# Attention and a gated feed-forward block in one kernel: turning some queries of batch 1 by DMA, turning 64-token tiles without their unused rows, and moving batch 2's scaling

## The chip, the cores and the metric

The kernel runs on one core of one Trainium2 chip. Times are device microseconds of that core; a profile is one execution of its own, and its span is about 2 us shorter than the time. A ratio is the mean time of one kernel's fast runs over the mean of the other's in the same rounds, so it is not quite the ratio of the medians that are quoted.

## The reference

```python
# 8 batches, 8 heads, 576 tokens, head dimension 64
def phi(x, c, s):                       # c, s: cos and sin of the token's position
    r = np.maximum(x, 0.0)
    return np.concatenate([r * c, r * s], axis=-1)
q_p, k_p = phi(q, cos_w, sin_w), phi(k, cos_w, sin_w)
kv  = np.einsum('bhsf,bhsd->bhfd', k_p, v)
num = np.einsum('bhsf,bhfd->bhsd', q_p, kv)
den = np.einsum('bhsf,bhf->bhs', q_p, k_p.sum(axis=2))[..., None] + 1e-06
x   = (num / den)                       # then [4608 tokens, 512]
g   = x @ w_gate                        # [512, 1536]
out = (gelu(g) * (x @ w_val)) @ w_out   # [1536, 512]
```

## The kernel before

A batch has 576 tokens: tiles 0 to 3 of 128 tokens and tile 4 of 64, which lie in the even rows of a 128-row tile. Scaled queries must be turned (features onto partitions) to be the stationary operand of the numerator; the normalised activations must be turned to feed the feed-forward block. Batches 0 and 1 turn theirs on TensorE, batches 2 to 7 by DMA. The feed-forward part runs in blocks of 512 tokens (block 0 has 576, the last 448), and the attention of the next batch is woven into a block. A "unit" is one call of `gv_unit`. To evacuate is to copy a result out of PSUM, the memory that TensorE writes.

```python
def turn_q(b, j0, j1):                  # queries, by DMA
    nc.sync.dma_start_transpose(out=qT[b % 2][:, j0:j1]..., in_=qp[:, j0:j1]...)

def numer_mm(b, t, bank, g, rows=128):
    for h in range(4 * g, 4 * g + 4):
        nc.tensor.matmul(ps[0:rows, bank + g, ...],
            lhsT=qT[b % 2][:, t, h, 0:rows], rhs=kv[b % 2][:, h, 0:D + 1], ...)

def turn_x(b, t, xb):                   # activations, by DMA
    if t < NJ:
        nc.sync.dma_start_transpose(out=xT[:, :, p0:p0 + 128], in_=xb2)
    else:                               # 64 tokens: turned with the unused rows, then picked out
        xr = rot.tile([128, CT, 128], BF16, name="xr")
        nc.sync.dma_start_transpose(out=xr, in_=xb2)
        nc.gpsimd.tensor_copy(xT[:, :, p0:p0 + 64], xr[:, :, 0:128:2])

def gv_unit(n, jt, c0, w, gb, vb):      # gate: 4 matmuls, gelu; value: 4 matmuls, product
    ...
```

The stretch that the change touches, the end of block 0 and the start of block 1 (`sq`, `sk` scale a tile of queries or keys; `o_tile` is an output tile; `x_by_pe`, `q_by_pe` turn on TensorE and copy out of PSUM):

```python
sq(4, 0, "v"), sq(4, 1, "s")
load_q(2)
...
o_tile(0, 1, 5)
q_by_pe(1, 2, 6, "v"); q_by_pe(1, 3, 7, "s")
cast_v(1, 0, 4, "v"); cast_v(1, 4, 8, "s")
load_v(2)
sq(0, ...), sq(1, ...), sq(2, 0, "v")          # of batch 2
o_tile(0, 2, 4)
q_by_pe(1, 4, 2, "v")
kv_half(1, 0, 6, "s"); kv_half(1, 1, 7, "v")
sq(2, 1, "s"), sq(3, 1, "s"), sq(4, 1, "s"); turn_q(2, 0, 3)
...
```

All transfers from `nc.sync` go through one queue, in program order; in this kernel's trace none of its 153 that were recorded landed before the one issued ahead of it.

## Time and profile before

| | before |
|---|---|
| time, median | 331.8 us (331.4 to 332.2) |
| span of the profile | 329.8 us |
| TensorE's share of the chain that ended last | 92% |
| from block to block (blocks 2 and on) | 33.77 us |
| block 2's first matmul | 86.69 us |

TensorE is the bound nearly everywhere, so a change is worth what it takes out of TensorE's stream or adds to it.

### The profile page before, as it was taken

Reading aid. Unit: us, or ns where it says so; the run is one execution under the profiler, and the core shown is the slowest. Engines: PE = TensorE matmul, PEld = TensorE weight load, DVE = VectorE, ACT = ScalarE, POOL = GpSimd, SP = SyncE. Lnnn points to the kernel's source line nnn. Section 1 sums busy time; section 2 is a strip of 40 time slices with the busy share of each in tenths; the row PEclk is TensorE's granted clock in tenths of the full one; section 3 lists DMA queues with packets and bytes.
Section 4 is the critical chain, followed back from the end, with each engine's and each line's share of the span. In section 5 each row is a group of like instructions: output and inputs, shape, how many; then the busy total and the mean of one; then the engine's idle time right before and its main releaser. Section 6 shows DMA issues by size and latency. Waiting matters only on the chain.

```text
span 329.8 us, 5965 instructions
## 1 busy us (share of the span) xinstructions
PE 319.8 (97%) x2245; PEld 170.7 (52%) x2280; DVE 173.3 (53%) x392; ACT 155.9 (47%) x283; POOL 19.7 (6%) x39
## 2 busy tenths in 40 slices
PE   7899999999999999999999999999999999999995
PEld 2578766655445444544454445444554444444443
DVE  5975477867664548354835474557545232222210
ACT  6864479683465247523752276226632223322321
POOL 2350010000100000000100010001000100000000
PEclk9999999999999999999999999999999999999998
DMA  7999999999289936994599549973723121000024
GB/s 231 264 170 207 220 342 329 299 242 312 54 137 265 319 80 114 274 329 84 94 279 298 119 84 218 370 121 73 167 49 80 22 59 32 32 34 33 33 64 97
DMA packets 84381, 54.66 MB, mean 166 GB/s; under 512 B 49408, under 2 KB 79872, under 8 KB 84352
## 3 DMA queue, kind: packets, MB, share of 16 engines
q1 hardware_dynamic: 78128, 49.10, 58.9%
q0 software_dynamic: 5792, 4.72, 9.4%
q10 hardware_dynamic: 432, 0.46, 0.4%
q8 instruction: 18, 0.29, 0.4%
q14 instruction: 11, 0.09, 0.1%
HBM read 37.75 MB, written 9.44 MB: 143 GB/s over the span
## 4 chain that ended last, share of the span: by engine, by line
PE 92%; DVE 2%; DMA 2%; ACT 1%; issue 1%; POOL 0%; DVEq 0%; POOLq 0%; ACTq 0%
PE ps L213 28%; PE ps L245 28%; PE ps L222 27%; PE ps L151 3%; PE ps L167 3%; DMA kf<-in_k_dram 2%; PE ps L310 1%; DVE qp L132 1%; PE ps L263 1%; ACT kp L134 1%; PE ps L329 1%; DVE kp L132 1%; ACT xT L332 0%; ACT gel L218 0%; DVE xb L182 0%
## 5 line engine op out<-in xcount | busy, mean ns | idle before, releaser
L226 DVE TENSOR_TENSOR hT<-gel,ps 128x512 bf16<-128x512 f32 (+5 forms) x130 | 76.9, 596 | 132.6 <-PE ps L222 126.7
L213 PE MATMUL ps<-xT,wg_sb 128*128 128x512 bf16 (+5 forms) x506 | 113.1, 342 | 1.5 <-ACT xT L332 0.5
L222 PE MATMUL ps<-xT,wv_sb 128*128 128x512 bf16 (+5 forms) x508 | 113.0, 342 | 0.8 <-DVE hT L226 0.4
L218 ACT ACTIVATE gel<-ps 128x512 f32<-128x512 f32 (+5 forms) x130 | 68.1, 525 | 78.2 <-PE ps L213 75.0
L245 PE MATMUL ps<-wo_sb,hT 128*128 128x512 bf16 x413 | 95.6, 379 | 0.6
L222 PEld LDWEIGHTS <-wv_sb 128*128 128x128 bf16 x520 | 48.8, 98 | 45.7 <-issue 0.5
L213 PEld LDWEIGHTS <-wg_sb 128*128 128x128 bf16 x520 | 47.0, 98 | 40.3 <-issue 1.2
L245 PEld LDWEIGHTS <-hT 128*128 128x128 bf16 x420 | 40.1, 98 | 45.4
L274 ACT COPY o_sb<-ps 128x512 f32<-128x512 f32 x35 | 20.5, 585 | 74.5 <-PE ps L245 70.2
L182 DVE TENSOR_TENSOR xb<-ps,rec 128x512 bf16<-128x512 f32 (+2 forms) x41 | 27.8, 678 | 1.5
L134 ACT ACTIVATE kp<-kf,sin_c 128x512 bf16<-128x512 f32 (+1 forms) x41 | 25.3, 680 | 1.0 <-DMA kf<-in_k_dram 1.0
L132 DVE TENSOR_SCALAR qp<-qf,cos_c 128x512 bf16<-128x512 f32 (+1 forms) x45 | 21.5, 521 | 0.7 <-DMA qf<-in_q_dram 0.7
L167 PEld LDWEIGHTS <-qT 128*128 128x128 bf16 (+1 forms) x320 | 15.2, 98 | 9.0 <-issue 1.7
L134 ACT ACTIVATE qp<-qf,sin_c 128x512 bf16<-128x512 f32 (+1 forms) x31 | 19.2, 665 | 0.7 <-DMA qf<-in_q_dram 0.7
L132 DVE TENSOR_SCALAR kp<-kf,cos_c 128x512 bf16<-128x512 f32 (+1 forms) x45 | 18.0, 450 | 1.4 <-DMA kf<-in_k_dram 1.4
L167 PE MATMUL ps<-kv,qT 128*128 128x65 bf16 (+1 forms) x320 | 16.7, 194 | 0.1
L206 POOL COPY xT<-xr 128x256 bf16<-128x256 bf16 x6 | 2.4, 400 | 204.0 <-DMA xr<-xb 204.0
L124 PE MATMUL ps<-junk 128*128 128x512 bf16 x34 | 10.7, 471 | 1.8 <-DVE par_i L101 1.7
L151 PEld LDWEIGHTS <-kp 128*128 128x128 bf16 x320 | 10.8, 97 | 2.4 <-issue 1.4
L151 PE MATMUL ps<-vx,kp 128*128 128x65 bf16 x320 | 11.1, 193 | 0.1
L138 ACT CAST vx<-vf 128x1280 bf16<-128x1280 f32 (+1 forms) x9 | 10.7, 1194 | 0.2 <-DMA vf<-in_v_dram 0.2
L231 POOL COPY hT<-hT 128x768 bf16<-128x768 bf16 x8 | 7.6, 946 | 38.1 <-DVE hT L226 38.1
(55 smaller groups left out, 93.5 us busy)
## 6 DMA issues: line engine op xcount, KB each, us to landing
out_dram<-o_sb SPq DMA_DIRECT2D x38, 128.0 KB, 2.4
qf<-in_q_dram SPq DMA_DIRECT2D x7, 640.0 KB, 5.9
kf<-in_k_dram SPq DMA_DIRECT2D x7, 640.0 KB, 7.7
out_dram<-o_sb SPq DMA_DIRECT2D x16, 256.0 KB, 3.5
vf<-in_v_dram SPq DMA_DIRECT2D x6, 640.0 KB, 9.3
qf<-in_q_dram SPq DMA_DIRECT2D x7, 512.0 KB, 4.7
kf<-in_k_dram SPq DMA_DIRECT2D x7, 512.0 KB, 6.4
vf<-in_v_dram SPq DMA_DIRECT2D x6, 512.0 KB, 8.4
```

The costliest lines, as they stand in the source:

```text
L124: nc.tensor.matmul(ps[:, bank, :], lhsT=junk[:, 0:128], rhs=junk, start=True, stop=True)
L132: nc.vector.tensor_scalar(d, s, col, 0.0, op0=ALU.mult, op1=ALU.max)
L134: nc.scalar.activation(d, s, AF.Relu, scale=col)
L151: nc.tensor.matmul(ps[:, bank, (h % 4) * (D + 1):(h % 4 + 1) * (D + 1)], lhsT=kp[:, j, h, :], rhs=vx[b % 2][:, j, h, 0:D + 1], start=(j == ...
L167: nc.tensor.matmul(ps[0:rows, bank + g, (h % 4) * (D + 1):(h % 4 + 1) * (D + 1)], lhsT=qT[b % 2][:, t, h, 0:rows], rhs=kv[b % 2][:, h, 0:D ...
L182: nc.vector.tensor_tensor(xb[0:rows, g0:g1], nd[:, :, :, 0:D], rec[0:rows, 0:n, :, None].to_broadcast([rows, n, 4, D]), op=ALU.mult,)
L213: nc.tensor.matmul(ps[:, gb, 0:w], lhsT=wg_sb[:, ct, jt * 128:(jt + 1) * 128], rhs=xT[:, ct, p0:p0 + w], start=(ct == 0), stop=(ct == CT - 1),
L218: nc.scalar.activation(gel[:, 0:w], ps[:, gb, 0:w], AF.Gelu)
L222: nc.tensor.matmul(ps[:, vb, 0:w], lhsT=wv_sb[:, ct, jt * 128:(jt + 1) * 128], rhs=xT[:, ct, p0:p0 + w], start=(ct == 0), stop=(ct == CT - 1),
L226: nc.vector.tensor_mul(hT[n % 2][:, jt, 64 + c0:64 + c0 + w], gel[:, 0:w], ps[:, vb, 0:w])
L245: nc.tensor.matmul(ps[:, bank, :], lhsT=hT[n % 2][:, jt, c0:c0 + 128], rhs=wo_sb[:, jt, :], start=(jt == 0), stop=(jt == JT - 1),)
L274: nc.scalar.copy(o_sb, ps[:, bank, :])
```

## The change

Three things are meant to help. Tiles 2 to 4 of batch 1's queries are turned by DMA, queued behind v, so that TensorE is spared 24 transposes. Tiles of 64 tokens use only their 64 columns in the numerator (at stride 2), so their result can be turned straight into place. Batch 2's query scaling must then wait for that DMA turn, and moves among block 1's first units.

```diff
-                lhsT=qT[b % 2][:, t, h, 0:rows],
+                lhsT=qT[b % 2][:, t, h, 0:128:2] if t == NJ and b else qT[b % 2][:, t, h, 0:rows],
@@ turn_x
-        if t < NJ: ...dma_start_transpose(out=xT[:, :, p0:p0 + 128], in_=xb2)
-        else: xr = ...; dma_start_transpose(out=xr, in_=xb2); gpsimd.tensor_copy(...)
+        rows = 128 if t < NJ else 64
+        nc.sync.dma_start_transpose(
+            out=xT[:, :, p0:p0 + rows], in_=xb[0:rows].rearrange("p g h d -> p (g h d)"))
@@
     sq(4, 0, "v"), sq(4, 1, "s")
+    turn_q(1, 2, 5)
     load_q(2)
@@
-    q_by_pe(1, 2, 6, "v")
-    q_by_pe(1, 3, 7, "s")
-    sq(0, 0, "v"), sq(0, 1, "s")  ... all of batch 2's sq, turn_q(2, ...), load_q(3)
-    q_by_pe(1, 4, 2, "v")
@@ now after x_by_pe(1, 0), x_by_pe(1, 1), numer(1, 3), numer(1, 4):
+    sq(0, ...)   sq(1, ...)   sq(2, ...), turn_q(2, 0, 3)
+    sq(3, ...), sq(4, ...), turn_q(2, 3, 5), load_q(3)
@@
-            turn_x(b, i - 1, numer(b, i - 1, 6))
+            turn_x(b, i - 1, numer(b, i - 1, 6, 128 if i <= NJ else 64))
```

More of the change, by code (lines that the diff above doesn't have):

```diff
@@ L199, in turn_x @@
         p0 = b * S + t * 128
-        xb2 = xb.rearrange("p g h d -> p (g h d)")
-        if t < NJ:
-            nc.sync.dma_start_transpose(out=xT[:, :, p0:p0 + 128], in_=xb2)
-        else:
-            xr = rot.tile([128, CT, 128], BF16, name="xr")
-            nc.sync.dma_start_transpose(out=xr, in_=xb2)
-            nc.gpsimd.tensor_copy(xT[:, :, p0:p0 + 64], xr[:, :, 0:128:2])
+        rows = 128 if t < NJ else 64
+        nc.sync.dma_start_transpose(
+            out=xT[:, :, p0:p0 + rows], in_=xb[0:rows].rearrange("p g h d -> p (g h d)"),
+        )
     def gv_unit(n, jt, c0, w, gb, vb, mid=()):
@@ L462 @@
     load_v(2)
-    sq(0, 0, "v"), sq(0, 1, "s")
-    sq(1, 0, "v"), sq(1, 1, "s")
-    sq(2, 0, "v")
     o_tile(0, 2, 4)
-    q_by_pe(1, 4, 2, "v")
     kv_half(1, 0, 6, "s")
     kv_half(1, 1, 7, "v")
-    sq(2, 1, "s"), sq(3, 1, "s"), sq(4, 1, "s")
-    turn_q(2, 0, 3)
     y0, y1 = new_xb(), new_xb()
@@ L479 @@
     norm(y1, 2, 0, 2)
-    sq(3, 0, "v"), sq(4, 0, "v")
-    turn_q(2, 3, 5)
-    load_q(3)
     o_part(0, 3, 5, 2, 6)
@@ L485 @@
     x_by_pe(1, 0, y0, 0, "s")
+    sq(0, 0, "v"), sq(0, 1, "s")
     o_part(0, 3, 5, 6, 9)
     x_by_pe(1, 1, y1, 1, "s")
+    sq(1, 0, "v"), sq(1, 1, "s")
     o_part(0, 3, 5, 9, 12)
     y3 = numer(1, 3, 2)
+    sq(2, 0, "v"), sq(2, 1, "s")
+    turn_q(2, 0, 3)
     gv_unit(1, 0, 0, 128, 0, 4)
@@ L495 @@
     y4 = numer(1, 4, 2, 64)
+    sq(3, 0, "v"), sq(4, 0, "v"), sq(3, 1, "s"), sq(4, 1, "s")
+    turn_q(2, 3, 5)
+    load_q(3)
     gv_unit(1, 1, 128, 128, 1, 5)
```

## The prediction

> **What bounds the kernel now.** I read the page first (busy shares, slices, chain), then the chain and the timeline from 44 to 90 us, where the change acts, then a table of stretches and the landings of the transfers.
>
> ```profile
> PE 319.8 (97%) x2245; PEld 170.7 (52%) x2280; DVE 173.3 (53%) x392; ACT 155.9 (47%) x283; POOL 19.7 (6%) x39
> PE   7899999999999999999999999999999999999995
> DMA  7999999999289936994599549973723121000024
> PE 92%; DVE 2%; DMA 2%; ACT 1%; issue 1%; POOL 0%; DVEq 0%; POOLq 0%; ACTq 0%
> ```
>
> TensorE holds 92% of the chain and is never under nine tenths after slice 3. A saving must therefore be matmul time removed or a TensorE gap closed. From block 2 on the chain repeats every 33.77 us (the 40 matmuls of the key-value product at 102.40, 136.18, 169.95, 203.72): pure matmul pace, where nothing off TensorE shows. Block 2 begins at 86.86: its first output tile starts at 90.31, after two units of 1.73.
>
> The second row to see is DMA. In the stretches (columns: us, busy of PE, PEld, DVE, ACT, POOL, clock, DMA share, GB/s):
>
> ```profile
> 50.00:62.00 12.00, 11.89 (x149) 7.88 (x150) 9.83 (x25) 9.79 (x17) 0.00 (x0) 1.00 1.02 353
> 62.00:70.00 8.00, 7.54 (x72) 5.01 (x71) 5.74 (x17) 5.99 (x13) 0.00 (x0) 1.00 1.21 187
> 70.00:81.00 11.00, 10.78 (x103) 5.86 (x104) 7.81 (x16) 5.49 (x10) 0.00 (x0) 1.00 1.17 346
> 81.00:85.00 4.00, 4.00 (x34) 2.10 (x33) 3.31 (x8) 1.20 (x2) 0.00 (x0) 1.00 0.72 110
> 88.00:92.00 4.00, 4.00 (x19) 1.85 (x19) 3.31 (x8) 2.78 (x5) 0.70 (x1) 1.00 0.00 0
> ```
>
> From 50 to 81 us the transfer queue has no free time: q, k, v of batch 2 (50 to 62), the two query turns of batch 2 (62 to 69.4), q, k, v of batch 3 (to 81). It falls idle only after 87. What ends this run of transfers are the turned activations of batch 2, which block 2's first matmul reads (its 512 tokens end inside tile 3 of batch 2):
>
> ```profile
> L202 SPq DMA_TRANSPOSE xT<-xb x4: 1188/1204/2103, 77.0 to 83.0; - x4
> DMA to landing us min/median/max: 2.4/3.5/5.9
> ```
>
> The first was issued at 76.95 and landed 5.9 later, at 82.7, because the loads of batch 3 were ahead of it. In the trace's landings the next two follow at 83.2 and 83.7; the fourth, issued at 82.96, is free of the queue and lands at 85.25. Block 2 starts at 86.86, so the slack is 1.6 us.
>
> **What the Trainium skill says.** "VectorE: DVE Perf Modes", The three transpose paths, gives 390 ns for a 128x128 transpose on TensorE and 1309 ns by DMA. Here pipelined ones cost far less on TensorE (0.89 us for 16, 56 ns each); by DMA, 24 blocks issued into an idle queue at 91.71 landed 6.8 us later. "DMA: Bandwidth & Descriptors", Issuing engines are not separate DMA queues, says that all DMAs share 16 engines and interleave; the trace agrees in that the 57.50 turn waited behind v. "TensorE: Matmul & The Clock Gate", Weight-path perf modes, says fast weight load needs all 128 columns. The trace shows 64-column loads at 110 ns against 98, but the same pace of matmuls (31 to 33 ns). "Advanced Engine Details and Errata", SBUF Cachelines, warns of strided reads; no weights of stride 2 are loaded in this trace, so their price is open.
>
> **The change, part by part.**
>
> (1) 24 TensorE transposes of batch 1 go.
>
> ```profile
> 51.68 0.89 PE ps L310 x16
> 55.16 0.45 PE ps L310 x8
> ```
>
> 0.89 + 0.45 = 1.34 us off the chain. The four copies out of PSUM go too: of VectorE 0.69 (tile 2) and 0.69 (tile 4), of ScalarE 1.01 (tile 3); both engines then finish the casts of v sooner, so the key-value product can follow at once.
>
> (2) In their place one DMA turn of tiles 2 to 4, issued when the last scaling ends, at 48.6. v of batch 1 lands at 49 to 50, so the turn moves from about 49.9. It is the same size as the one at 91.71 (3 tiles), 5.6 to 6.8 us to landing in two steady blocks: landing 54.2 to 55.4. Its first reader, the numerator of tile 2, is at 58.8 now and 57.4 after: hidden, with 2 us to spare.
>
> (3) But it takes the queue. 3072 rows of 256 bytes move at 0.84 to 1.13 per ns, 2.7 to 3.6 us, and where a turn follows loads the packets show a pause of about 1.3 us (62.5 to 63.5, 81 to 82). I take 4.2 us. The load of q of batch 2 comes behind it on the same issuer, whose turn instruction holds it some 4 us:
>
> ```profile
> 48.26 1.31 SPq L78 DMA_DIRECT2D qf<-in_q_dram  x2
> 57.50 7.03 SPq L142 DMA_TRANSPOSE qT<-qp  x1
> ```
>
> q of batch 2 then starts moving at 54.2 instead of 50.0, and everything behind it in the gapless queue slides by as much. Queue-bound landings of batch 2's activations become 82.7 + 4.2 = 86.9, 87.4, 87.8, and the fourth about 88.3. Block 2's first matmul then waits until 88.3 to 88.4 against 86.86: **+1.5 us** at that point, whatever TensorE won before.
>
> (4) Batch 2's query scaling moves. q of batch 2 lands about 54.2 + 4.4 = 58.6 (it took 4.4 from first packet, 50.0, to the first reader's start, 54.38). VectorE asks for it about 59.6: no wait, perhaps a short one. ScalarE is worse: five scalings of 0.72 (3.6 us) ran at 54.7 to 58.6 and now sit among the evacuations and gelus of the first units. Laying them out in program order from 58.7: evacuation of x 1 by 60.6, store copy by 61.9, third scaling 62.6, two gelus 63.2, evacuations of x 2 and 3 with a gelu between 64.7, last two scalings 66.1, gelu 66.4. The unit that reuses that gelu's bank began at 65.65 before and cannot now before 66.4. So the 1.34 us of (1) is gone by 66 and 0.8 us more with it. This is not added to (3): both must be past before block 2, and the later (3) sets it.
>
> (5) The 64-row numerator in batches 2 to 7. Eight matmuls keep their pace, but a change of the array's shape costs TensorE its run-ahead loading:
>
> ```profile
> 63.63 0.33 PEld L167 LDWEIGHTS <-qT 128*64 128x64 bf16 x8
> 64.00 0.23 PEld L213 LDWEIGHTS <-wg_sb 128*128 128x128 bf16 x4
> ```
>
> Around this only such group of batch 1, the matmul starts are 149 ns apart going in (55 inside the group before) and 126 coming out (33 inside): 0.094 each, 0.19 for both. Six batches: 6 x 0.19 = **+1.1 us**, all in the matmul-bound blocks. If loading at stride 2 is slow, up to 48 x 30 ns = 1.4 more; I put no size on it.
>
> (6) Turning 64 rows straight into place takes away six GpSimd copies of 0.40 and half the rows of six small turns. Their data is read a block later: 0.
>
> Sum: 331.8 + 1.5 + 1.1 = 334.4. I shade it to 334.0, since the slide in (3) rests on one queue's estimate.
>
> **Rivals.**
>
> (A) The author's case: all 1.34 us kept, the turn and the moved scalings hidden, no cost in (5): 330.5. For it: TensorE is the bound, 92% of the chain. Against: the DMA row of nines up to 81 us and the 1.6 us of slack at block 2, and the measured 0.19 of a shape change.
>
> (B) ScalarE sets block 1 but the queue does not bind block 2 (say the turn takes only 2.7 us with no pause; then the fourth landing is at 86.8 and block 2 is on time): 331.8 + 0.8 + 1.1 = 333.7. For it: the pauses in the packets come irregularly. Against: four turns in the trace had one.
>
> (C) The slide is larger, since the turn holds the issuer for 7 us as at 57.50, and the turned queries of batch 2 come close to their first reader (landing about 72 now predicted, reader at 74.7): with 6 us of slide block 2 starts at 90, 331.8 + 3.3 + 1.1 = 336.2; slow strided loads would add to it.
>
> (D) Scaling is hidden and the queue is not bound, only (1) and (5): 331.8 - 1.34 + 1.1 = 331.6.
>
> **Range and chances.** The four rivals lie between 330.5 and 336.2; I weigh the main path and (B) most, (C) and (D) less, (A) least. Range 331.2 to 336.6. Two per cent are 6.6 us, more than any sum here: within 2% 0.95, slower 0.04, faster 0.01.
>
> **What would show it.** (1): 56 transposes of queries instead of 80. (2): no wait of the numerators for the DMA turn around 57. (3): the batch 2 activations landing at 87 to 88.5, a TensorE gap of 1 to 2 us before block 2's first matmul that names this DMA, and the q, k, v loads of batch 2 starting 4 us later. (4): ScalarE busy without gaps from 59 to 70, and TensorE gaps there of 1 to 2 us in all that name the gelu. (5): a period of 33.96 instead of 33.77 from block to block. I am wrong if the period is unchanged or longer by over 0.3, if block 2 starts before 86.9, or if TensorE waits for the turned queries.

## More of the kernel before

A transfer has landed when the last of its completion signals has come.

The prediction shows the lines. The one it left out is block 2's first matmul itself (timeline, TensorE; start, duration, engine and line):

```profile
86.69 1.03 PE L213 MATMUL ps<-xT,wg_sb 128*128 128x512 bf16 x4
```

## The result, and the profile after

The changed kernel took 335.78 us in the median of five runs (335.39 to 338.39), against 331.8; the ratio is 1.0133 (95% interval 1.0093 to 1.0174). It is 4.0 us slower, inside the predicted range (331.2 to 336.6), and nearly twice the predicted loss of 2.2.

The page of the changed kernel, the lines that answer to those of before (busy time, TensorE and DMA in 40 slices, the chain by engine):

```profile
PE 320.5 (96%) x2221; PEld 169.5 (51%) x2256; DVE 169.0 (51%) x390; ACT 154.6 (46%) x282; POOL 16.9 (5%) x33
PE   7899999799799999999999999999999999999995
DMA  7999999999858955994499449992924021000024
PE 86%; DMA 5%; DVE 3%; ACT 3%; issue 2%; SPq 1%; POOL 0%; DVEq 0%; ACTq 0%; POOLq 0%
```

TensorE's row has two new dips, in its eighth and eleventh slice (58 to 67 and 83 to 92 us). Everything else of the row is as it was. The stretches of the changed kernel (columns as in the prediction):

```profile
50.00:62.00 12.00, 10.57 (x122) 6.42 (x123) 8.41 (x23) 6.71 (x12) 0.00 (x0) 1.00 1.00 276
62.00:70.00 8.00, 7.54 (x70) 5.16 (x71) 5.86 (x18) 7.39 (x18) 0.00 (x0) 1.00 1.14 302
70.00:81.00 11.00, 10.83 (x104) 5.87 (x105) 7.57 (x16) 5.63 (x11) 0.00 (x0) 1.00 1.07 273
81.00:85.00 4.00, 4.00 (x32) 1.96 (x31) 2.86 (x8) 0.94 (x3) 0.00 (x0) 1.00 1.08 360
88.00:92.00 4.00, 2.62 (x12) 1.29 (x14) 2.16 (x5) 1.21 (x2) 0.82 (x1) 1.00 0.20 40
```

From 81 to 85 the queue now moves 360 GB/s where it moved 110: loads that were over by 81 are still running. TensorE loses 1.3 us from 50 to 62 and 1.4 us from 88 to 92. The transfer queue's own timeline shows who stands in front (SPq is the issuer, the duration is how long the instruction held it):

```profile
48.89 3.73 SPq L142 DMA_TRANSPOSE qT<-qp  x1
52.67 1.29 SPq L78 DMA_DIRECT2D qf<-in_q_dram  x2
62.90 10.26 SPq L142 DMA_TRANSPOSE qT<-qp  x2
```

q of batch 2 is issued at 52.67 instead of 48.26. In the trace the new turn lands at 54.5, in good time for its reader (tile 2's numerator, at 57.1). But q lands too late for its readers:

```profile
59.83 0.72 ACT L134 ACTIVATE qp<-qf,sin_c 128x512 bf16<-128x512 f32 x1 [1.30 <-DMA qf<-in_q_dram]
61.08 0.38 PE L210 MATMUL ps<-xT,wg_sb 128*128 128x128 bf16 x4 [0.79 <-ACT xT L329]
62.17 0.38 PE L219 MATMUL ps<-xT,wv_sb 128*128 128x128 bf16 x4 [0.71 <-ACT o_sb L271]
62.96 0.38 PE L210 MATMUL ps<-xT,wg_sb 128*128 128x128 bf16 x4 [0.18 <-ACT gel L215]
```

The brackets are the idle time ahead of an instruction and what ended it. ScalarE stands 1.30 us waiting for q; the evacuations and gelus behind that scaling come late, and TensorE waits for each in turn. Counted from the starts of the matmuls, TensorE's gaps there are 0.95, 0.88, 0.35 and 0.11 us, 2.3 in all.

At block 2, the four turns of batch 2's activations, who waited for them, and the first matmul:

```profile
L201 SPq DMA_TRANSPOSE xT<-xb x4: 1218/1956/3652, 77.9 to 85.7; - x4
  DVE xb L182: 3.1, 1
  PE ps L210: 2.0, 1
DMA to landing us min/median/max: 3.4/5.4/9.7
```
```profile
89.33 1.02 PE L210 MATMUL ps<-xT,wg_sb 128*128 128x512 bf16 x4 [1.95 <-DMA xT<-xb]
```

The first turn takes 9.7 us from issue to landing instead of 5.9; the four land at 87.5, 88.0, 88.5 and 89.1. TensorE was ready at 87.2 and starts at 89.33: block 2 begins 2.64 us later than before.

Last, the block period, by the 40 matmuls of a batch's key-value product in the chain, before and then after:

```profile
102.40 1.36 PE ps L151 x40
136.18 1.36 PE ps L151 x40
```
```profile
105.03 1.36 PE ps L151 x40
139.03 1.36 PE ps L151 x40
```

33.78 us became 34.00. The span's growth of 3.9 us is then: 2.64 at block 2; four more blocks of 0.225 (0.90); 0.15 in the last batch; and one wait of 0.2 for VectorE in batch 6's numerator at 216.8.

### The profile page after: what moved, and what is told of

Same layout as the page of the kernel before. It is cut to its first block, busy times and chain, and to the rows that moved or that the text cites. A ratio compares the mean times of both kernels' runs of the same rounds, so it can differ in the third digit from the quotient of the medians.

```text
span 333.7 us, 5904 instructions
## 1 busy us (share of the span) xinstructions
PE 320.5 (96%) x2221; PEld 169.5 (51%) x2256; DVE 169.0 (51%) x390; ACT 154.6 (46%) x282; POOL 16.9 (5%) x33
## 4 chain that ended last, share of the span: by engine, by line
PE 86%; DMA 5%; DVE 3%; ACT 3%; issue 2%; SPq 1%; POOL 0%; DVEq 0%; ACTq 0%; POOLq 0%
PE ps L210 27%; PE ps L242 26%; PE ps L219 26%; PE ps L151 3%; PE ps L167 3%; DMA qf<-in_q_dram 2%; DMA kf<-in_k_dram 2%; DMA xT<-xb 1%; DVE qp L132 1%; ACT kp L134 1%; PE ps L260 1%; PE ps L307 1%; ACT qp L134 1%; DVE kp L132 1%; DVE xb L182 1%
## 5 line engine op out<-in xcount | busy, mean ns | idle before, releaser
L228 POOL COPY hT<-hT 128x768 bf16<-128x768 bf16 x8 | 6.8, 852 | 248.7 <-DVE hT L223 248.7
L132 DVE TENSOR_SCALAR qp<-qf,cos_c 128x512 bf16<-128x512 f32 (+1 forms) x45 | 18.9, 463 | 0.3 <-DMA qf<-in_q_dram 0.3
L163 ACT CAST kv<-ps 128x260 bf16<-128x260 f32 x15 | 5.7, 378 | 7.7 <-PE ps L151 7.7
```

The source lines that it names most:

```text
L132: nc.vector.tensor_scalar(d, s, col, 0.0, op0=ALU.mult, op1=ALU.max)
```

## The experiments

The theory: one queue carries everything, so the added turn delays all behind it (the waits at 60 and at 89); and a 64-column tile switches the array's shape, which costs TensorE 0.2 us per batch. The rivals: weights at stride 2 are slow; VectorE, held by a buffer, delays block 2; the moved scaling is what costs. All runs gave a correct result unless said otherwise.

### e2: the 64-column tile alone

```diff
 (on the kernel before)
-    lhsT=qT[b % 2][:, t, h, 0:rows],
+    lhsT=qT[b % 2][:, t, h, 0:128:2] if t == NJ and b > 1 else qT[b % 2][:, t, h, 0:rows],
 and turn_x, numer(..., 64) as in the change
```

> The kernel before with one part of the change alone: the numerator of tile 4 in batches 2 to 7 with 64 columns at stride 2, and the turn of 64 rows straight into place. My theory (each switch of the array's shape costs 0.1 us, two per batch, nothing else in the part costs or wins): the block period goes from 33.77 to about 34.0 us and the time from 331.8 to 333.0 to 333.3. Rival, that the part is free or wins (fewer rows turned, no copy by GpSimd) and the whole loss of the changed kernel lies in block 1: 331.8 or less, period 33.77.

333.18 us in the median (332.42 to 334.87) against 331.47, ratio 1.0064 (1.0033 to 1.0095). The period is 34.00 us in each block. The part that looked like pure saving is a loss. The weight loads of one such tile, kernel before and then the changed one (timeline of weight loads, block 3):

```profile
118.28 0.50 PEld L167 LDWEIGHTS <-qT 128*128 128x128 bf16 x8
```
```profile
121.21 0.33 PEld L167 LDWEIGHTS <-qT 128*64 128x64 bf16 x8 [0.42 <-issue]
```

With 128 columns the first load slips in under the matmul before it, and no idle time is shown. With 64 columns (128\*64 is the shape) the loads stand idle for 0.42 us first. The starts of the matmuls show what of this counts: 0.09 us going into the shape (309 ns from start to start where 216 is usual) and 0.09 coming out (126 where 33 is). Another 0.03 lies right behind these two gaps (53 ns where 29 is usual, 226 where 215 is), which makes up the 0.225 by which the period grew.

### e6: the same 64 columns, side by side

```diff
 (on the changed kernel; a wrong result on purpose)
-    lhsT=qT[b % 2][:, t, h, 0:128:2] if t == NJ and b else qT[b % 2][:, t, h, 0:rows],
+    lhsT=qT[b % 2][:, t, h, 0:rows],
```

> The changed kernel, but the 64 columns of tile 4 are read side by side and not at stride 2 (a wrong result on purpose: the wrong queries). My theory, that the shape of the array costs and not the stride: same time as the changed kernel, 335.8, same period of 34.0 us, gaps of 0.10 us going in and coming out. Rival, that weights at stride 2 are slow: the period falls to 33.8 and the time by 1.0 to 1.4 us.

The result is wrong. 336.61 us in the median (334.91 to 338.43), ratio 1.0152 (1.0100 to 1.0203). The period is 34.00 us again, with the same two gaps of 0.09. So the stride costs nothing; the shape does. The four runs fall into two pairs: 334.9 and 335.3 at a mean clock of 1.0, and 338.0 and 338.4 at 0.995. The last section comes back to that.

### e3: one load moved out of the way

```diff
 (on the changed kernel)
-            put(5 + s, L(load_v, b + 1))
+            if n > 1:
+                put(5 + s, L(load_v, b + 1))
         for i in range(5):
             put(6 + (n == 1) + s + i, L(attn_step, b, i + 1))
+            if n == 1 and i == 3:                  # behind the turn of tile 3
+                put(6 + 1 + s + i, L(load_v, b + 1))
```

> The changed kernel with one load moved in the transfer queue: v of batch 3 is issued behind the turn of tile 3 of batch 2 instead of ahead of the four turns. My theory, that the full queue delays the turned activations and those hold block 2: the turns land by 86 and block 2 starts at about 87.2 us when TensorE is ready for it, not at 89.3; the time falls from 335.8 to 333.5 to 334.0. Rivals: if ScalarE's moved scalings or the wait of VectorE for a buffer were what delays block 2, its start stays at 89 and the time at 335.8.

333.53 us (332.87 to 334.38), ratio 1.0059 (1.0038 to 1.0081). That is 2.2 us under the changed kernel's median (of other rounds; its ratio was 1.0133), by the order of the queue alone. The turns land at 85.2 to 86.6, and block 2's first matmul has no wait in front of it:

```profile
87.44 1.03 PE L210 MATMUL ps<-xT,wg_sb 128*128 128x512 bf16 x4
```

### e4: a fifth buffer for the activations

```diff
 (on the changed kernel)
-        return rot.tile([128, 2, 4, D], BF16, name="xb", bufs=4)
+        return rot.tile([128, 2, 4, D], BF16, name="xb", bufs=5)
```

> The changed kernel with five buffers for the normalised activations instead of four, so that tile 4 of batch 2 need not wait for the turn of its tile 0: it removes the 3.07 us in which VectorE waits for that turn at 84.5 to 87.6. My theory: TensorE waits for the last turn itself, so block 2 still starts at 89.3 and the time stays at 335.8 (at most 0.3 less). Rival, that VectorE's held products are what TensorE waits for: block 2 starts near 87.2 and 2 us are won.

336.72 us (334.66 to 337.16), ratio 1.0142 (1.0108 to 1.0175). VectorE's wait is gone, TensorE's is not:

```profile
85.10 0.68 DVE L182 TENSOR_TENSOR xb<-ps,rec 64x512 bf16<-64x512 f32 x1
```
```profile
90.40 0.81 PE L210 MATMUL ps<-xT,wg_sb 128*128 128x512 bf16 x3 [2.50 <-DMA xT<-xb]
```

The 3.1 us of VectorE was the longest wait in the list of that transfer, and it cost nothing. The buffer rival falls.

### e7: the price of the turn alone

```diff
 (on the kernel before)
     load_v(2)
     ...
+    nc.sync.dma_start_transpose(                    # 24 blocks of weights, into unused columns
+        out=xT[:, 0, 1536:4608].rearrange("p (a t) -> p a t", t=128),
+        in_=wg_sb[:, 0:2].rearrange("p c j -> p (c j)"),
+    )
     turn_q(2, 0, 3)
```

> The kernel before with one transfer added and nothing else touched: a turn of the size of the one that the change adds (24 blocks of 128 by 128, of weights, into columns of the activations that are not yet in use), issued behind v of batch 2. It measures the price of the turn to the transfer queue alone. My theory: everything behind it lands 3 to 4.5 us later, the fourth turn of batch 2's activations at 87.5 to 88.5, block 2 starts 1.3 to 2.3 us later than in the kernel before (86.7), the time is 333.0 to 334.0 and the period of 33.77 us stays. Rival, that the queue has slack or that the extra turn runs beside the loads: 331.5.

333.23 us (332.88 to 334.76), ratio 1.0058 (1.0038 to 1.0078). With no instruction of the four compute engines changed, block 2 waits:

```profile
89.95 1.02 PE L213 MATMUL ps<-xT,wg_sb 128*128 128x512 bf16 x4 [2.76 <-DMA xT<-xb]
```

The turns land at 88.2 to 89.7 in that profile and the period stays 33.77. The profiled execution was the slowest of the four (334.76), so its 3 us are at the upper end; the median lost 1.7.

### e5: TensorE turns the queries again, the rest of the change stays

```diff
 (on the changed kernel)
-    turn_q(1, 2, 5)
+    q_by_pe(1, 2, 6, "v"); q_by_pe(1, 3, 7, "s")    # after o_tile(0, 1), as before
+    q_by_pe(1, 4, 2, "v")                           # after o_tile(0, 2), as before
 (and tile 4 of batch 1 is read at 0:rows again)
```

> The changed kernel with tiles 2 to 4 of batch 1 turned by TensorE again (the DMA turn and its place in the queue are gone, the 24 transposes and four copies are back); batch 2's scaling stays among block 1's first units and tile 4 stays 64 columns wide. My theory: q of batch 2 lands at 54 again, so the waits for it at 59.8 go; ScalarE's moved scalings still cost some 0.5 to 0.9 us against the kernel before in block 1; block 2 starts at 87.2 to 87.9; time 333.3 to 334.3, of which 1.2 for the 64 columns. Rival, that the moved scaling and not the turn is the main loss of block 1 and block 2: 335 or more.

332.82 us (332.70 to 332.96), ratio 1.0036 (1.0024 to 1.0049), and the least scatter of all. q is there when ScalarE asks for it (timeline of ScalarE):

```profile
59.41 0.72 ACT L134 ACTIVATE qp<-qf,sin_c 128x512 bf16<-128x512 f32 x1
60.03 0.58 ACT L329 COPY xT<-ps 128x512 bf16<-128x512 bf16 x1
```

From batch 1's key-value product to batch 2's took 16.97 us, against 16.55 before: the moved scaling costs 0.4 us by itself. The 64 columns (period 34.00) cost most of the rest. Block 2 does not wait. The time lies half a microsecond under what was expected.

### e1: tile 4 back at 128 columns

```diff
 (on the changed kernel) turn_x and numer of batches 2 to 7 as in the kernel before
```

> The changed kernel with tile 4 of batches 2 to 7 handled as in the kernel before (128 columns, turned whole, copied by GpSimd). My theory: the period returns to 33.77 us, the wait at block 2 stays (a start at 89 to 90.5), the time falls by 1.0 to 1.3 us, to 334.5 to 335.5. Rival, that the two parts of the loss are not independent: the gain is under 0.5 us.

335.35 us (335.18 to 336.89), ratio 1.0125 (1.0102 to 1.0148). The period returns to 33.78. The median is only 0.4 us under the changed kernel's, which by itself looks like the rival; but the two are of different rounds, and e4 and e6, which differ from the changed kernel in nothing that counts, took 336.7 and 336.6. In this profile the turns landed at 88.4 to 89.9 and block 2 began at 90.17, 0.8 later than in the changed kernel's: a stretch that ends with a transfer scatters with that transfer. All four runs of e1 also show a lowered mean clock (0.993 to 0.995), where the changed kernel's lay between 0.990 and 1.0; the last section says what that is. The period settles the 64 columns' cost; this run's time does not.

### e8: the two costs taken away together

```diff
 (on e1) load_v as in e3
```

> The changed kernel with two of its costs taken away at once: tile 4 of batches 2 to 7 back at 128 columns, and v of batch 3 behind the turns of batch 2's activations. What is left of the change is the DMA turn of batch 1's queries and the moved scaling. My theory (the costs add): no wait at block 2, period 33.77 us, and only the waits for q of batch 2 in block 1 (2 to 3 us in all) less the 1.34 us of transposes: 332.0 to 332.9, that is 0.5 to 1.3 us slower than the kernel before. Rival, that the parts were not the whole of the loss: over 333.5; rival, that the turn wins once the queue is put right: under 331.3.

333.36 us (331.56 to 334.07), ratio 1.003 (0.9995 to 1.0066). The period is 33.78 and block 2 does not wait. The time lies above what was expected: the waits for q in block 1 remain (gaps of 0.94, 0.88, 0.35 and 0.10 us), and in the profiled execution the clock was halved for 3.4 us right behind them, as in e1. The runs part along that line: three with a mean clock of 0.995 took 333.6 to 334.1 us, three with 0.998 to 1.0 took 331.6 to 333.1, 332.4 in the mean, which is what was expected. The turn of batch 1's queries wins nothing even with the later queue put right.

### b1: no shape but 128 by 128 anywhere

```diff
 (on the kernel before)
-            xs[t] = numer(0, t, 0, 128 if t < NJ else 64)
+            xs[t] = numer(0, t, 0)
-    y4 = numer(1, 4, 2, 64)
+    y4 = numer(1, 4, 2)
 q_evac copies all 128 columns; x_by_pe turns 128 rows and copies every second column
```

> The kernel before with the two remaining tiles of 64 tokens (tile 4 of batches 0 and 1) given 128 columns and 128 rows in the numerator and in the transposes, so that the array's shape is never switched. My theory: eight switches of 0.09 us go, 0.75 us, and eight transposes become 64 columns wider, 0.2 us back: 0.5 us faster than the kernel before, if these switches are not hidden in waits of block 0 and 1 anyway. Rival, that they are hidden there: no difference.

331.78 us (331.32 to 333.55) against 331.52, ratio 1.0012 (0.9993 to 1.003). No gain. Blocks 0 and 1 have waits for ScalarE and VectorE of their own; a saving inside them was not visible here.

### b2 and b3: a version with the queue in mind

```diff
 (b2, on b1)
     load_q(2)
+    turn_q(1, 2, 5)                  # behind q of batch 2, not ahead of it
-    q_by_pe(1, 2..4)
     sq(0), sq(1) of batch 2 before the numerators; sq(2) to sq(4) later, as in the change
     y2 = numer(1, 2), y3 = numer(1, 3) after the last o_part
     load_v as in e3
 (b3, on b2)
-    kv_half(1, 1, 7, "v")
+    kv_half(1, 1, 7, "s")
-    y3 = numer(1, 3, 2)              # ahead of block 1's first two units
+    y3 = numer(1, 3, 2)              # behind them
```

> A try at a version that beats both: the DMA turn of batch 1's queries stays, but q of batch 2 is issued ahead of it; the numerators of tiles 2 and 3 come after the last part of the output tile, so that the later landing of the turn (about 58.5 us) is not waited for; two of batch 2's scalings go back before the numerators; v of batch 3 goes behind the turns of batch 2; all tiles are 128 columns wide. My theory: 24 transposes less (1.3 us) with no wait for q, period 33.77 us, block 2 starts near 86: 330.3 to 331.2. Rival, that the one queue is too full for any extra turn in this stretch (something else then arrives late): 332 or more.

b2: 331.72 us (330.55 to 332.15) against 331.67, ratio 0.9987 (0.9952 to 1.0023). It no longer loses, and does not win: the transposes' 1.3 us went into waits of 0.3 to 0.8 us for VectorE and ScalarE in block 1's first units.

> The reordered try once more, with two of its remaining TensorE waits taken out: the second half of the key-value product is evacuated by ScalarE ahead of batch 2's scalings (it waited behind VectorE's scalings), and the numerator of tile 3 comes after block 1's first two units, so that their products are not held behind its normalisation. My theory: some 0.5 to 0.9 us less than the reordered try (331.7), 330.6 to 331.3, that is at most 0.3 per cent faster than the kernel before, within what five rounds can just tell. Rival, that ScalarE or the landing of the turn takes over the wait: 331.7 again.

b3: 330.94 us (330.18 to 332.05) against 331.75, ratio 0.9974 (0.9945 to 1.0002). In the median it is 0.8 us faster than the kernel before, and it beats the changed kernel by far, but the interval just touches 1: likely a small win, not shown.

## Why the prediction was right or wrong

It was right in direction and range, and in the mechanism of its two main terms, (3) and (5); the sum of its steps was too small, and the shading from 334.4 to 334.0 went the wrong way.

Step (1), the 24 transposes: right. TensorE reaches batch 1's key-value product at 54.08 instead of 55.45, 1.37 us earlier. (The four copies that it speaks of are three, those that it lists.)

Step (2), the turn itself hidden: right. It landed at 54.5 (predicted 54.2 to 55.4) and no numerator waited.

Step (3), the slide of the queue: right in mechanism, mis-sized. It was put at +1.5 and is 2.64. Three pieces make the difference. The fourth turn landed at 89.1, not 88.3; of this 0.5 is the slide itself, 4.7 us for the first turn where 4.2 had been taken. The matmul started 0.25 us after that landing, where at most 0.1 had been allowed. And block 2 had begun at 86.69 before, not at 86.86, a figure worked out from the chain where the timeline had it directly. So the slack before was 1.3 us, not 1.6: the landings in the prediction are those of a transfer's first completion signal, and the last one of the fourth turn came at 85.36, not 85.25. e7 shows the slide without the rest of the change, e3 takes it away, and e4 removes the other wait that stood in the same list.

Step (4), ScalarE: the mechanism was half right. The prediction let q land at 58.6 with "no wait, perhaps a short one"; its readers started at 59.83. Behind the turn the loads restart slowly: in the packet records 68 KB of q moved from 54 to 55 us, where the full queue moves some 350. So the first wait was for q, and the pile-up of scalings came behind it; the predicted sign of a ScalarE without gaps from 59 us on did not appear. e5 separates the two: without the turn the moved scalings cost 0.4 us. The end was milder than predicted all the same: batch 2's key-value product starts 0.3 us later than before, not 0.8. And it was right that this is not added to (3).

One agreement in its part on the skill is weak: the turn that waited behind v came from the same issuer, so it does not test a sentence about different issuers, and no run here does.

Step (5), the 64 columns: right. 0.225 per block instead of 0.19. One of the six batches lies before the wait at block 2 and is swallowed by it, so five count: 1.05 us. e6 closes what the step left open, the stride.

Rival (A), that the transposes' saving is kept, is refuted; so are (B) and (D), which need a queue with slack. (C), the larger slide, is nearest in size: 336.2 for 335.8. But this is luck: it saw the reason in an issuer held for 7 us and turned queries that come late; the issuer was held for 3.73, and no query was late.

## What to carry to other kernels

When one queue has no free time, an added transfer is paid by whatever lands last in it, not by its own reader: find that landing, and its slack against the engine that reads it, before giving work to the DMA. Saving columns by giving one small matmul group another array shape can cost more than the columns. And of two waits for the same transfer, the longer one (VectorE, 3.1 us) can cost nothing while the shorter (TensorE, 2.0 us) is the loss: take one away and look.

## What the Trainium skill lacked or had wrong

- "TensorEngine Tiling (Array Packing)", Key Properties, says that a change of tiling mode drains TensorE; it gives no price. Here the passage between 128 and 64 columns, with no tiling asked for, cost 0.094 us each way (149 ns from matmul to matmul going in, where 55 is the rule, and 126 coming out, where 33 is), and 0.225 us per block in all. That this is the drain of the page is likely and not shown.
- "TensorE: Matmul & The Clock Gate", Part 1, says that the clock halves after an idle window of about 3.4 us, and its rule table asks for no gaps above about 3 us. (Part 1 also tells of another kernel whose short idles between groups of matmuls made the clock oscillate, without their length.) In e1 it halved for 3.41 us after waits of 1.2 and 0.9 us only; the changed kernel with nearly the same waits kept its clock, and so did e3 with the same. The stretches of e1 (the column 1.00 or 0.50 is the granted clock):

```profile
60.00:62.60 2.60, 0.82 (x13) 0.57 (x11) 2.24 (x6) 2.54 (x5) 0.00 (x0) 1.00 1.02 344
62.60:66.00 3.40, 3.40 (x37) 3.05 (x35) 1.45 (x6) 2.88 (x8) 0.00 (x0) 0.50 1.07 385
```

  TensorE was busy for 0.82 of 2.60 us, then ran 3.4 us at half speed. e8 did so at 63.2 us, e6 at 91.7 us behind its wait at block 2, and b1 at 19.3 us in block 0. The traces show what tells these apart. In every profile the changes of the clock lie whole multiples of 3.413 us apart (in e1 58.03, 3.41 and 266.24 us: 17, 1 and 78). Cut into windows of that length, TensorE was busy for only 1.09 to 1.75 us of the window just before each of the four halvings (in e1 1.63 us, from 59.20 to 62.61). In the changed kernel the same waits were divided between two windows, busy for 2.34 and 2.81 us. Of the windows without a halving behind them one was as low (1.74 us, its wait at block 2); all others had 1.88 or more. Four halvings are few, so this is a reading and not a tested rule. What a halving costs shows in b1, whose one such run took 333.55 us where the other five took 331.3 to 331.9, about half of 3.4 us more. It is not the whole scatter of the kernels with waits: e4 took 334.7 and 336.7 us at the full clock.
- "Advanced Engine Details and Errata", X-Bar Transpose (TRN2), puts turns at 350 to 400 GB/s, as fast as plain transfers. ("DMA: Bandwidth & Descriptors" has 261 GB/s for a non-contiguous case; this one is contiguous.) Here 24 blocks (786 KB) took from 50.0 to 53.8 us in the changed kernel, 207 GB/s by that count, and no half microsecond of a turn was above 146 KB; and the loads behind it restarted slowly (68 KB in the first us). No page has the pause of about 1.3 us that stands in several turns queued behind loads (68.0 to 69.5 us in the changed kernel).
- "TensorE: Matmul & The Clock Gate", Weight-path perf modes, ties fast weight load to 128 columns. Weights of 64 columns kept the pace of 31 to 33 ns per matmul all the same, at stride 2 as at stride 1 (e6, period 34.00 in both).
